# Cosine of a three-stage fused kernel: quarter turn added before rounding, absolute value dropped

## The chip, the cores and the metric

One core of a Trainium2 chip runs the whole program. The metric is device time in microseconds (us) of one execution, median of 3 runs. The core's engines run their own instruction streams in order and wait for each other by semaphores: TensorE (PE in the profile, its weight loads PEld), VectorE (DVE), ScalarE (ACT), GpSimd (POOL), and SyncE (SP), which here only starts DMAs.

## The reference, cut to what matters

```
x  = chunked softmax attention(q, k, v)        # 8 batches, 8 heads, 576 tokens in chunks of 64
x  = x as 4608 tokens by 512
h  = x @ w_in            # 4608 x 2048
g  = h * cos(h)          # the line that the change touches
x  = g @ w_out           # 4608 x 512
out = ((x @ w1) * (x @ w2)) @ w3 @ w_out2
```

All arrays are fp32. The kernel multiplies w3 by w_out2 once, in parts that it calls folds, so the last layer needs a single product per tile.

## The kernel before, in words

Every matrix product is made of three matmuls (function mm3, lines 106 to 108): each operand is split into a high part, rounded to the PE's fp32r format by a ScalarE copy, and a low part, which is the difference. The tokens form 9 tiles of 512, and the 2048 hidden columns form 8 groups of 256. A group of one tile is one step of the main loop; there are 72 steps, and in each of them two tiles of 128 x 512 hidden values are made, called d and e (variable `which` 0 and 1).

The steps run in two passes. Pass 1 takes tiles 0 to 8 with groups 0 to 4 and makes attention for the next tile on the way; its sums over groups are stored as x2a. Pass 2 takes groups 5 to 7 of every tile, adds the stored sums (line 600, `x2a<-x2a,acc`, four VectorE additions after a tile's third group), and makes the folds on the way. After pass 2 comes the second feed-forward layer, in which no cosine is taken.

The first 10 steps (class Plain) multiply by 16 blocks; d and e stay in PSUM, and the tile's PSUM bank is free again when VectorE has read it for the last time, at line 562. All later steps use a scheme with seven block products instead of eight (class Seven): step1 makes x1 (ScalarE copies it out of PSUM, line 481), step2 makes d (VectorE, line 489), step5 makes parts of e and the rest of d (lines 499, 501), step3 the rest of e (line 508). d and e then lie in SBUF.

The cosine of d or e is a chain over two engines, with one tile t:

- chain_t (line 547, ScalarE): t = h/2pi, written as a whole number (int32)
- chain_r (line 552, VectorE): t = h/2pi - t
- chain_cos (lines 557 and 558, ScalarE): absolute value, then sine with a scale and with half_pi (a column of 128 values) as the bias
- chain_g (line 562, VectorE): t = t * h
- split_g (lines 570 and 571): high part on ScalarE, low part on GpSimd, into g, from which x2_mm makes the sums over groups one step later

No scheduler moves anything: the order on every engine is the order of the code. It is set by strings, one letter per action, such as ORDER1PE and ORDER3: "1", "2", "5", "3" are the products, "a"/"c" chain_t of d and e, "A"/"C" chain_r, "b"/"d" chain_cos, "B"/"D" chain_g, "s" split_g of the step before, "x"/"y" x2_mm, "q" a piece of attention or a fold, "o" one of the seven operands of the next tile (a split, lines 101 and 102), "l", "m", "h", "r" the four parts of the conversion of one weight tile (raw weights come in by DMA, line 116; the first to read them are lines 253 on ScalarE and 263 on VectorE).

ScalarE's exponential (line 375, attention) and its sine are in different function tables, so a table load stands ahead of each exponential and of each first sine after one.

Of the kernel before, what the change touches and what calls it, by code (L numbers as in the profile page):

```python
# [11 lines left out]
I32 = mybir.dt.int32  # L12
U32 = mybir.dt.uint32
AF = mybir.ActivationFunctionType
# [15 lines left out]
INV2PI = 1.0 / (2.0 * math.pi)  # L30
TWO_PI = 2.0 * math.pi
# [25 lines left out]
def chunk_attention_two_ffn(  # L57
# [13 lines left out]
    nc = tc.nc  # L71
# [20 lines left out]
    half_pi = cpool.tile([P, 1], F32, name="half_pi")  # L92
# [451 lines left out]
    def chain_t(i, h, which):  # L544

        rr[i, which] = t = wk.tile([P, TT], F32, tag="t", name="t")
        nc.scalar.activation(t.bitcast(I32), h, AF.Copy, scale=INV2PI)  # L547

    def chain_r(i, h, which):

# [3 lines left out]
    def chain_cos(i, which):  # L554

        t = rr[i, which]
        nc.scalar.activation(t, t, AF.Abs)  # L557
        nc.scalar.activation(t, t, AF.Sin, scale=-TWO_PI, bias=half_pi)  # L558

    def chain_g(i, h, which):  # L560
        t = rr[i, which]
# [194 lines left out]
    with tc.manual_schedule():  # L756
# [34 lines left out]
        for i in range(NG):  # L791
# [35 lines left out]
            for op in order_of(i, nth, end):  # L827
# [24 lines left out]
                elif op == "r":  # L852
                    st_lo()
                elif op in "1253PQ":
                    getattr(z, "step" + op)()
                elif op in "ac":
                    chain_t(i, z.d if op == "a" else z.e, "ac".index(op))
                elif op in "AC":
                    chain_r(i, z.d if op == "A" else z.e, "AC".index(op))
                elif op in "bd":  # L860
                    chain_cos(i, "bd".index(op))
                elif op in "BD":
                    chain_g(i, z.d if op == "B" else z.e, "BD".index(op))
                elif op == "q":
                    if i < iA and nth < 4:
                        att_tok(steps[20 * n + 5 * nth + n_q], False)
                    elif i >= iB + FOLD and fq < 4 * FB2:
                        need(("w3", fq // 2), *(("wo2", j) for j in range(FB2)))
                        fold(fq // 4, fq % 4)
                        fq += 1  # L870
                        if fq == 4 * FB2:
                            load_wf(0)
                            load_wf(1)
                    n_q += 1
                elif op in "ST":
                    x_sums("ST".index(op))
                elif op == "o":
                    if i < GA and not n_o:
                        x_plain()
                    x_op((z.done if i < GA or i >= 2 * GA else OPS)[n_o], n + 1 if ps == 0 else None)  # L880
                    n_o += 1
# [138 lines left out]
```

## Time and profile before

| what | value |
|---|---|
| median of 3 runs | 1510.13 us (1508.39 to 1510.74) |
| the profiled execution | 1515.81 us |
| its span, first to last instruction | 1514.0 us |
| busy share of the span | PE 96%, PEld 83%, DVE 73%, ACT 51%, POOL 17% |
| mean granted TensorE clock | 0.994 |

A busy time is the time in which at least one instruction of an engine runs. Matmuls of one engine overlap, since the next is started while the one before drains, so a PE that is 96% busy can still lose time between two starts. In a row of the timeline, what stands in square brackets is how long the engine sat idle ahead of it, and which engine's instruction released it. A table of waits gives for each pair of waiting and releasing instruction the total, the number of times and the longest.

### The profile page before, as it was taken

Reading aid. Unit: us, or ns where it says so; the run is one execution under the profiler, and the core shown is the slowest. Engines: PE = TensorE matmul, PEld = TensorE weight load, DVE = VectorE, ACT = ScalarE, POOL = GpSimd, SP = SyncE. Lnnn points to the kernel's source line nnn. Section 1 sums busy time; section 2 is a strip of 40 time slices with the busy share of each in tenths; the row PEclk is TensorE's granted clock in tenths of the full one; section 3 lists DMA queues with packets and bytes.
Section 4 is the critical chain, followed back from the end, with each engine's and each line's share of the span. In section 5 each row is a group of like instructions: output and inputs, shape, how many; then the busy total and the mean of one; then the engine's idle time right before and its main releaser. Section 6 shows DMA issues by size and latency. Waiting matters only on the chain.

```text
span 1514.0 us, 26149 instructions
## 1 busy us (share of the span) xinstructions
PE 1455.7 (96%) x9996; PEld 1251.1 (83%) x9996; DVE 1099.8 (73%) x1844; ACT 766.9 (51%) x1317; POOL 262.0 (17%) x194
## 2 busy tenths in 40 slices
PE   4789999999999999999999989999999999999998
PEld 4678778888888888888888878898888888888886
DVE  6986798888988887767777777776665656656553
ACT  3777788888888876555555555321122013004002
POOL 0222222222222222222222112120100200200000
PEclk9999999999999999999999999999999999999999
DMA  7664555565665626998889774596434542641501
GB/s 235 204 210 133 188 173 204 188 228 166 227 218 165 229 88 248 363 328 299 309 308 326 252 282 127 196 367 238 152 140 154 190 153 90 228 157 59 210 33 56
DMA packets 122814, 307.39 MB, mean 203 GB/s; under 512 B 13633, under 2 KB 25665, under 8 KB 121537
## 3 DMA queue, kind: packets, MB, share of 16 engines
q1 hardware_dynamic: 122688, 305.71, 58.3%
q8 instruction: 79, 1.29, 0.4%
q14 instruction: 47, 0.38, 0.1%
HBM read 210.50 MB, written 95.16 MB: 202 GB/s over the span
## 4 chain that ended last, share of the span: by engine, by line
PE 65%; ACT 12%; DVE 12%; DMA 7%; issue 2%; POOL 1%; SPq 0%; DVEq 0%; ACTq 0%; POOLq 0%
PE ps_hh L106 9%; PE acc L107 8%; PE acc L106 8%; PE acc L108 8%; PE ps_hh L108 8%; PE ps_hh L107 8%; PE ps_aa L107 4%; PE ps_aa L106 4%; PE ps_aa L108 4%; ACT t L558 2%; DMA sd<-raw 2%; ACT L375 2%; ACT t L557 2%; ACT L558 1%; POOL ex L384 1%
## 5 line engine op out<-in xcount | busy, mean ns | idle before, releaser
L571 POOL TENSOR_TENSOR g<-t,g 128x512 fp32r<-128x512 f32 x144 | 196.2, 1384 | 591.6 <-ACT g L570 517.2
L106 PE MATMUL acc<-g,w 128*128 128x512 f32 x576 | 228.6, 397 | 0.0
L107 PE MATMUL acc<-g,w 128*128 128x512 f32 x576 | 227.1, 394 | 0.1
L108 PE MATMUL acc<-g,w 128*128 128x512 f32 x576 | 225.0, 391 | 0.0
L108 PE MATMUL ps_hh<-T,w 128*128 128x256 f32 (+1 forms) x616 | 182.2, 296 | 6.3 <-DVE w L199 6.2
L106 PE MATMUL ps_hh<-T,w 128*128 128x256 f32 (+1 forms) x616 | 185.3, 301 | 0.5 <-ACT x L481 0.5
L107 PE MATMUL ps_hh<-T,w 128*128 128x256 f32 (+1 forms) x616 | 181.8, 295 | 0.0
L108 PEld LDWEIGHTS acc<-g,w 128*128 128x128 f32 x576 | 108.5, 188 | 23.3
L107 PEld LDWEIGHTS acc<-g,w 128*128 128x128 f32 x576 | 108.9, 189 | 22.3 <-POOL g L571 3.0
L108 PEld LDWEIGHTS ps_hh<-T,w 128*128 128x128 f32 x616 | 118.6, 193 | 9.4 <-DVE w L199 6.9
L106 PE MATMUL ps_hh<-B,w 128*128 128x256 f32 (+1 forms) x396 | 120.4, 304 | 5.3 <-DVE t L562 3.3
L106 PEld LDWEIGHTS acc<-g,w 128*128 128x128 f32 x576 | 108.9, 189 | 19.7
L106 PEld LDWEIGHTS ps_hh<-T,w 128*128 128x128 f32 x616 | 118.6, 192 | 6.4 <-ACT x L481 0.9
L745 ACT ACTIVATE phl<-e 128x512 fp32r<-128x512 f32 x32 | 20.2, 633 | 201.5 <-DVE e L743 201.5
L107 PEld LDWEIGHTS ps_hh<-T,w 128*128 128x128 f32 x616 | 118.6, 193 | 3.2
L107 PE MATMUL ps_hh<-B,w 128*128 128x256 f32 (+1 forms) x396 | 116.6, 294 | 0.0
L108 PE MATMUL ps_hh<-B,w 128*128 128x256 f32 (+1 forms) x396 | 116.4, 294 | 0.0
L558 ACT ACTIVATE t<-t,half_pi 128x512 f32<-128x512 f32 x144 | 104.3, 724 | 4.0
L106 PE MATMUL acc<-wf,phl 128*128 128x512 f32 x252 | 98.2, 390 | 1.5 <-DVE o L688 1.5
L107 PE MATMUL acc<-wf,phl 128*128 128x512 f32 x252 | 98.1, 389 | 0.0
L108 PE MATMUL acc<-wf,phl 128*128 128x512 f32 x252 | 98.0, 389 | 0.0
L547 ACT ACTIVATE t<-d 128x512 int32<-128x512 f32 x62 | 38.9, 628 | 115.8 <-DVE d L501 115.8
(200 smaller groups left out, 3513.8 us busy)
## 6 DMA issues: line engine op xcount, KB each, us to landing
w<-sd SPq DMA_DIRECT2D x159, 512.0 KB, 5.6
sd<-raw SPq DMA_DIRECT2D x104, 256.0 KB, 4.5
s<-sd SPq DMA_DIRECT2D x43, 256.0 KB, 4.8
qk<-in_q_dram SPq DMA_DIRECT2D x36, 256.0 KB, 4.4
qk<-in_k_dram SPq DMA_DIRECT2D x36, 256.0 KB, 4.5
vt<-in_v_dram SPq DMA_DIRECT2D x72, 128.0 KB, 3.1
x2a<-x2o SPq DMA_DIRECT2D x36, 256.0 KB, 2.6
x2a<-x2a SPq DMA_DIRECT2D x36, 256.0 KB, 6.0
```

The lines of the kernel that those rows point to most:

```text
L106: nc.tensor.matmul(ps, a[0], b[0], start=first, stop=False)
L107: nc.tensor.matmul(ps, a[0], b[1], start=False, stop=False)
L108: nc.tensor.matmul(ps, a[1], b[0], start=False, stop=last)
L375: nc.scalar.activation(ex, ex, AF.Exp, scale=SCALE)
L384: (nc.vector if early else nc.gpsimd).tensor_tensor(out=ex, in0=ex, in1=rc.unsqueeze(2).to_broadcast([P, 2 * HP, 64]), op=ALU.mult)
L547: nc.scalar.activation(t.bitcast(I32), h, AF.Copy, scale=INV2PI)
L557: nc.scalar.activation(t, t, AF.Abs)
L558: nc.scalar.activation(t, t, AF.Sin, scale=-TWO_PI, bias=half_pi)
L571: nc.gpsimd.tensor_tensor(out=lo, in0=r, in1=f32(hi), op=ALU.subtract)
L745: nc.scalar.activation(t[:, 0], e0, AF.Copy)
```

## The change

The whole number is now that of h/2pi + 1/4 and no longer that of h/2pi, which is a bias of 0.25 in the ScalarE copy that makes it. The rest h/2pi - t then lies between -3/4 and 1/4 of a turn and no longer between -1/2 and 1/2, and the sine of 2pi times the rest plus half_pi is the cosine for any of these values, with arguments from -pi to pi. The absolute value is left out, and the sine's scale changes its sign. There are two absolute values a step, 144 in all.

```diff
     def chain_t(i, h, which):
         rr[i, which] = t = wk.tile([P, TT], F32, tag="t", name="t")
-        nc.scalar.activation(t.bitcast(I32), h, AF.Copy, scale=INV2PI)
+        nc.scalar.activation(t.bitcast(I32), h, AF.Copy, scale=INV2PI, bias=0.25)

     def chain_cos(i, which):
         t = rr[i, which]
-        nc.scalar.activation(t, t, AF.Abs)
-        nc.scalar.activation(t, t, AF.Sin, scale=-TWO_PI, bias=half_pi)
+        nc.scalar.activation(t, t, AF.Sin, scale=TWO_PI, bias=half_pi)
```

The instruction order of PE, VectorE, GpSimd and SyncE is the same in both kernels, row for row; only ScalarE's differs, by the 144 rows that are gone. All lines after 557 have a number lower by one in the changed kernel: the sine is line 557 there, split_g 569 and 570.

The first place is on ScalarE in the last step of the second tile in pass 1, where the seven operands of the next tile are made between the cosines. B11, B21, T1 to T4 and B22 are these operands, xf and spare what they are made from, t_2137 and t_2139 the tiles t of d and e. Before:

```order
L101 ACTIVATE B21_167<-xf_164 128x512
L557 ACTIVATE t_2137<-t_2137 128x512
L558 ACTIVATE t_2137<-t_2137,half_pi_163 128x512
L101 ACTIVATE T2_168<-spare_165 128x512
L101 ACTIVATE T1_169<-spare_165 128x512
L557 ACTIVATE t_2139<-t_2139 128x512
L558 ACTIVATE t_2139<-t_2139,half_pi_163 128x512
L101 ACTIVATE T3_170<-xf_164 128x512
L101 ACTIVATE B22_171<-xf_164 128x512
L101 ACTIVATE T4_172<-xf_164 128x512
L481 ACTIVATE x1_2203<-ps_hh_2196 128x256
```

The same place on ScalarE in the changed kernel, where the two tiles t are called t_2119 and t_2121:

```order
L101 ACTIVATE B21_167<-xf_164 128x512
L557 ACTIVATE t_2119<-t_2119,half_pi_163 128x512
L101 ACTIVATE T2_168<-spare_165 128x512
L101 ACTIVATE T1_169<-spare_165 128x512
L557 ACTIVATE t_2121<-t_2121,half_pi_163 128x512
L101 ACTIVATE T3_170<-xf_164 128x512
L101 ACTIVATE B22_171<-xf_164 128x512
L101 ACTIVATE T4_172<-xf_164 128x512
L481 ACTIVATE x1_2183<-ps_hh_2176 128x256
```

Both absolute values are gone, and five splits and the copy of x1 each stand one or two places nearer to the front.

The second place is on ScalarE in pass 2, in the first step after a tile's end. d and e are the hidden values, x1 the first product of the next step, g what x2_mm reads. Before:

```order
L547 ACTIVATE t_8244<-d_8188 128x512
L547 ACTIVATE t_8260<-e_8241 128x512
L557 ACTIVATE t_8244<-t_8244 128x512
L558 ACTIVATE t_8244<-t_8244,half_pi_163 128x512
L557 ACTIVATE t_8260<-t_8260 128x512
L558 ACTIVATE t_8260<-t_8260,half_pi_163 128x512
L481 ACTIVATE x1_8311<-ps_hh_8304 128x256
L570 ACTIVATE g_8328<-t_8244 128x2x256
```

The same place on ScalarE in the changed kernel:

```order
L547 ACTIVATE t_8148<-d_8092 128x512
L547 ACTIVATE t_8164<-e_8145 128x512
L557 ACTIVATE t_8148<-t_8148,half_pi_163 128x512
L557 ACTIVATE t_8164<-t_8164,half_pi_163 128x512
L481 ACTIVATE x1_8213<-ps_hh_8206 128x256
L569 ACTIVATE g_8230<-t_8148 128x2x256
```

The two sines follow each other directly; each waits for VectorE's subtraction of its own tile, as the absolute value did. The copy of line 547 has the same operands in both kernels, so the bias of 0.25 is part of the instruction and no further column that is read.

## Rows read from the trace of the kernel before

**Rows 1.** Page: busy us of each engine, share of the span, instructions:

```profile
PE 1455.7 (96%) x9996; PEld 1251.1 (83%) x9996; DVE 1099.8 (73%) x1844; ACT 766.9 (51%) x1317; POOL 262.0 (17%) x194
```

**Rows 2.** Busy us of PE, PEld, DVE, ACT, POOL by stage; then clock, DMA share, GB/s:

```profile
0.00:130.00 130.00, 95.44 (x1030) 83.04 (x1031) 101.48 (x185) 82.73 (x141) 21.02 (x21) 0.96 0.58 189
...
200.00:560.00 360.00, 355.77 (x3442) 303.86 (x3441) 312.63 (x575) 295.10 (x497) 102.20 (x81) 1.00 0.58 192
...
640.00:890.00 250.00, 242.43 (x1428) 215.34 (x1427) 182.18 (x307) 130.75 (x230) 50.55 (x38) 0.99 0.88 307
```

**Rows 3.** Tile t: durations in ns (min/median/max), first and last start in us:

```profile
L557 ACT ACTIVATE t<-t x144: 612/617/637, 43.4 to 959.4; 128x512 f32<-128x512 f32 x144
L558 ACT ACTIVATE t<-t,half_pi x144: 721/724/728, 45.3 to 960.1; 128x512 f32<-128x512 f32 x144
...
L547 ACT ACTIVATE t<-d x62: 615/632/637, 192.3 to 954.6; 128x512 int32<-128x512 f32 x62
```

**Rows 4.** Waits over the whole span: us in total, times, longest us:

```profile
DVE t L562 <- ACT t L558: 37.4, 70, 3.1
...
PE ps_hh L106 <- DVE d L489: 6.8, 5, 3.0
```

**Rows 5.** Timeline of PE at six places: start, duration, idle ahead:

```profile
70.78 0.39 PE L108 MATMUL ps_hh<-T,w 128*128 128x256 f32 x1 [3.11 <-DVE w L199]
...
103.94 0.58 PE L108 MATMUL ps_hh<-T,w 128*128 128x256 f32 x1 [3.12 <-DVE w L199]
...
128.81 0.39 PE L106 MATMUL ps_hh<-B,w 128*128 128x256 f32 x1 [0.57 <-DVE t L562]
...
185.79 0.39 PE L106 MATMUL ps_hh<-B,w 128*128 128x256 f32 x1 [1.03 <-ACT x L481]
...
676.46 0.39 PE L106 MATMUL ps_hh<-B,s 128*128 128x256 f32 x1 [1.20 <-DVE d L489]
...
886.16 0.58 PE L106 MATMUL ps_hh<-B,s 128*128 128x256 f32 x1 [2.96 <-DVE d L489]
```

**Rows 6.** Timeline of ACT at a tile's end in pass 2:

```profile
669.42 0.63 ACT L547 ACTIVATE t<-e 128x512 int32<-128x512 f32 x1 [0.16 <-DVE e L508]
670.03 0.64 ACT L557 ACTIVATE t<-t 128x512 f32<-128x512 f32 x1
670.69 0.72 ACT L558 ACTIVATE t<-t,half_pi 128x512 f32<-128x512 f32 x1
...
671.97 0.72 ACT L558 ACTIVATE t<-t,half_pi 128x512 f32<-128x512 f32 x1
```

**Rows 7.** Timeline of DVE at the same place:

```profile
670.09 0.69 DVE L552 SCALAR_TENSOR_TENSOR t<-e,t 128x512 f32<-128x512 f32 x1
...
672.73 0.69 DVE L562 TENSOR_TENSOR t<-t,e 128x512 f32<-128x512 f32 x1 [0.58 <-ACT t L558]
673.34 2.47 DVE L600 TENSOR_TENSOR x2a<-x2a,acc 128x512 f32<-128x512 f32 x4
675.73 0.68 DVE L489 TENSOR_TENSOR d<-x,ps_hh 128x512 f32<-128x512 f32 x1
```

**Rows 8.** Waits of PEld from 200 to 560 us:

```profile
PEld ps_s L361 <- ACT xf L409: 1.6, 6, 0.3
```

**Rows 9.** Timeline of DVE in the first tile:

```profile
46.06 0.69 DVE L562 TENSOR_TENSOR t<-t,ps_hh 128x512 f32<-128x512 f32 x1 [0.33 <-ACT t L558]
```

**Rows 10.** Waits of PE from 570 to 965 us:

```profile
PE ps_hh L106 <- ACT x L481: 0.4, 1, 0.4
```

**Rows 11.** Waits of DVE from 570 to 965 us:

```profile
DVE cw L263 <- DMA raw<-in_w_dram: 22.3, 5, 5.2
```

**Rows 12.** Busy us and clock (third number from the end) in three short stretches:

```profile
71.00:74.00 3.00, 3.00 (x52) 2.80 (x52) 2.97 (x7) 1.68 (x3) 0.00 (x0) 1.00 0.44 147
...
104.00:107.00 3.00, 3.00 (x14) 3.00 (x15) 1.08 (x2) 0.47 (x1) 0.00 (x0) 0.50 0.94 328
...
886.00:892.00 6.00, 5.84 (x20) 5.16 (x21) 3.93 (x8) 2.71 (x5) 0.00 (x0) 0.50 1.03 406
```

## The prediction

> **What bounds the kernel now.** I read the page first: PE is busy 96% of the span, ScalarE 51% [rows 1]. The change takes work from ScalarE alone, so its worth is not ScalarE's busy time but the places where PE stands still because a cosine came late.
>
> Next the busy times by stage [rows 2]. From 200 to 560 us, where most cosines of pass 1 are made, ScalarE is busy 295 of 360 us and VectorE 313, but PE is idle for only 4.2. From 640 to 890 us PE idles 7.6 us, and in the first 130 us it idles 34.6. The last absolute value starts at 959.4 us [rows 3], so the remaining 555 us of the span have no part in this.
>
> Then the waits [rows 4]. VectorE waits 37.4 us in 70 places for a sine. This is the direct effect of the cosine's length, yet PE shows waits for few of those places. What PE waits for by way of VectorE is the first sum of the seven-product scheme (line 489, d): 6.8 us in five places, all in pass 2. The last view is the timeline around each idle piece of PE, to see whether an absolute value stands in the chain ahead of it [rows 5 to 7].
>
> **What one absolute value costs.** It lasts 617 ns [rows 3]; on the engine it takes 670.69 - 670.03 = 0.66 us from start to start [rows 6]. 144 of them by 0.62 to 0.66 us are 89 to 95 us of ScalarE, about an eighth of its work. Nothing is put in their place. The copy that rounds gets a bias: the trace has no such copy with a bias, so its cost is bounded by the two nearest rows, 632 ns for the copy without and 724 ns for the sine, which reads its bias from a column. The instruction order shows no second operand on the copy, so I take 0; the other end, 0.09 us a copy, would take 0.18 us at each place below where two copies stand in the chain. Below 0 it can't be, as the copy does all that it did. The sine now gets arguments from -pi to pi. All 144 last 721 to 728 ns whatever their data, so I take no change. The table loads stay as they are, 63 between sine and exponential in either order.
>
> **Where it lies on PE's path.** I go through the places in order of weight.
>
> *Tile ends in pass 2.* VectorE multiplies both tiles by their cosines, makes four additions to x2a (2.47 us) and only then the d that PE waits for [rows 7]. Now: the second sine starts at 671.97, its product at 672.73. After: the first sine can start when the second copy has left ScalarE, at 669.42 + 0.63 = 670.05, and lasts 0.72; the second sine waits for VectorE's subtraction, over at 670.09 + 0.69 = 670.78, and ends at 671.50, so the product starts at about 671.53. That is 1.2 us earlier. VectorE has no other wait from there to d, so d is ready 1.2 us earlier, and PE, which idles 1.20 us there [rows 5], loses all of it. The five idle pieces of PE are 1.20, 0.39, 1.09, 1.20 and 2.96 us; their sum is the 6.8 us of the table of waits. The fifth, at 886.16, is preceded by the fourth, which brings PE to it 1.2 us sooner; its releaser gets the same 1.2 us, so its length stays and I count nothing. The four others give 1.18 + 0.39 + 1.09 + 1.18 = 3.8 us.
>
> *End of the second tile, 185.79 us.* Two absolute values stand ahead of five splits and of x1 on ScalarE, and PE idles 1.03 us [rows 5]. ScalarE gives 1.3 us there, but VectorE must still do its splits and then read e out of PSUM, and it had only 0.43 + 0.35 = 0.78 us of waits to give up, and 0.1 more in front. I take 0.9.
>
> *Pass 1, 200 to 560 us.* Once in each tile the attention scores wait for a PSUM bank that ScalarE empties (xf) behind both sines: 1.6 us in six places [rows 8], of which some 0.06 us each is there at any such turn. I take 1.2. All the rest of this stage counts nothing: PE is idle 4.2 us in 360, so the cover that hides the saved 75 us of ScalarE there is PE itself.
>
> *First tiles.* At 128.81 PE idles 0.57 us for a product that waits for a sine [rows 5], with one absolute value in the chain: 0.5. In the first tile PE waits for VectorE's low parts of the weights at 70.78 and 103.94 [rows 5], and of VectorE's own waits there the cosine owns 0.33 us at 46.06 [rows 9] and as much again in the third step. I take 0.7, between 0.3 and 1.5.
>
> *The turns to the next tile at 568 and 930 us.* There PE waits directly for x1, behind two absolute values: 0.4 us at 930 [rows 10] and about half of that at 568, and the d behind it another 0.2 to 0.3 each. I take 1.0 for both.
>
> The sum is 3.8 + 0.9 + 1.2 + 0.5 + 0.7 + 1.0 = 8.1 us. The profiled execution took 1515.81 us (span 1514.0 and 1.8 around it), so it would take 1507.7. It is 5.7 us, 0.4%, above the median of the three timed runs; I carry the difference over to the median: 1510.1 - 8.1 = 1502.0 us. Less than 0.2%, some 3 us, can't be told from no change in a measurement of this kernel.
>
> **Rivals.**
>
> *More than that: the clock too.* [...] At 886 it was 0.50 for 5.84 us of work, 20 matmuls, which at full clock would have been about 2.9 us. If the pieces at 886 and 103.94 fall a little shorter, or just elsewhere, up to 2.9 + 1.5 = 4.4 us come on top: 1497.6 us. The same chance can turn against us at 70.78. [...]
>
> *Less: another wait takes the place.* In pass 2 VectorE waits 22.3 us in five places for raw weights [rows 11], with DMA busy 88% of that stage [rows 2]. If these loads keep their times, PE, now earlier, waits for them instead, and the 3.8 us are given back; in the first tiles VectorE's own work may take back the rest. What is left is 1 to 2 us: 1508.6. For it: the DMA share. Against it: SyncE issues these loads in order behind work that PE and VectorE release, which all comes earlier by as much.
>
> *Slower: raw weights later.* VectorE handles the conversion of raw weights in front of the sums that PE needs. PE has 0 to about 1 us in hand at these five places. If the earlier x2d stores and operand loads crowd the raw loads so that each lands more than 2 us later against PE, 5 x 2 less some 2 in hand eats the 8.1 us; with 3 us each the kernel is slower by about 5: 1515. For it speaks only the DMA share of 88%; against it, that the order of all DMAs is the same and nothing is added.
>
> *The bias costs as much as a column.* Then 0.18 us go at six or seven places, 1.2 us in all: 1503.2, inside the forecast.
>
> **How the numbers follow.** My forecast, 8.1 us less with its own range of 1498 to 1506 (each term between a half and one and a half, the bias's upper end in it): 0.60. The clock on top: 0.12. Less, given back: 0.21. Slower: 0.05. The bias as a column: 0.02. Faster by over 0.2% are the first, the second, the last and a little of the third: 0.76. Within 0.2%: the rest of the third and a bit of the fourth, 0.19. Slower: 0.05. The range for 8 in 10 goes from 1497 (most of the clock's case) to 1509.5 (the larger part of the third).
>
> **What the profile after would show.** ScalarE busy about 677 us, with no row of absolute values and the same 64 table loads, and the copy still at 615 to 637 ns. VectorE's waits for sines down from 37.4 to below 15 us. The idle pieces of PE for d at the four tile ends near 0, that at 886 about as long as before, and the one for x1 at the end of the second tile down to some 0.2 us. From 200 to 560 us PE idles about 3 us in place of 4.2, and the length of a step stays the same. I am wrong in the main step if PE's idle pieces at the tile ends stay, or if those for raw weights grow by what these lose; wrong on the bias if the copy gets longer; wrong on the clock if stretches at 0.50 come or go.

## The result, and the profile after

| | before | after | ratio of times, 95% interval |
|---|---|---|---|
| timed together, first | 1510.43 us (1508.39 to 1511.39, 4 runs) | 1494.84 us (1492.33 to 1496.78, 4 runs) | 0.989 [0.987, 0.991] |
| timed again | 1510.43 us (17 runs) | 1499.68 us (1492.60 to 1501.15, 6 runs) | 0.9912 [0.9889, 0.9934] |
| and again | 1510.05 us (11 runs) | 1498.40 us (1492.38 to 1499.47, 6 runs) | 0.9915 [0.9893, 0.9938] |

By the medians the change is worth 11 to 16 us. The forecast was 8.1 us, and the lower end of its range, 1497.0, lies 2 us above the first median. The two later medians lie inside the range, and so does that of all 16 runs, 1497.4. How good the forecast was is therefore read from the stages below and not from the medians. The profiled execution took 1492.33 us (span 1490.5).

Page of the kernel after, answering to [rows 1]:

```profile
PE 1444.5 (97%) x9996; PEld 1247.3 (84%) x9996; DVE 1094.4 (73%) x1844; ACT 687.4 (46%) x1173; POOL 264.7 (18%) x194
```

ScalarE lost 144 instructions and 79.5 us of busy time. TensorE's busy time fell by 11.2 us although its 9996 matmuls are the same, so a busy time holds more than work.

Tile t in the kernel after (ns min/median/max), answering to [rows 3]:

```profile
L557 ACT ACTIVATE t<-t,half_pi x144: 702/711/727, 42.2 to 937.5; 128x512 f32<-128x512 f32 x144
...
L547 ACT ACTIVATE t<-d x62: 612/632/635, 184.8 to 933.3; 128x512 int32<-128x512 f32 x62
```

The copy that rounds has its bias now and the same median as before, 632 ns. The sine is not longer for its wider arguments, 711 ns where it was 724 [rows 3].

Waits of VectorE in the kernel after, over the whole span (total us, times, longest), answering to [rows 4, 11]:

```profile
DVE d L489 <- ACT g L569: 33.8, 31, 2.2
...
DVE cw L263 <- DMA raw<-in_w_dram: 19.0, 5, 4.9
...
DVE t L561 <- ACT t L557: 3.2, 5, 2.6
```

The wait for sines went from 37.4 us in 70 places to 3.2 in 5. At line 489 VectorE now waits longer for ScalarE, 33.8 us where it was 14.0, but PE's waits for the d that is made there did not grow: over the whole span they are 3.3 us in three places where they were 6.8 in five. The wait for raw weights did not grow either.

For the rest, both kernels are cut into stages at the same seven matmuls (the 9996 matmuls have one order, so the nth of one kernel is the nth of the other). Stage lengths in us:

| stage, by the times of before | before, two profiles | after, three profiles | change | forecast |
|---|---|---|---|---|
| up to 110 | 110.2, 110.2 | 104.0, 110.4, 106.3 | see below | -0.7 |
| 110 to 200, second tile | 89.86, 89.83 | 88.49, 88.42, 88.46 | -1.4 | -1.4 |
| 200 to 560, rest of pass 1 | 360.04, 360.01 | 353.72, 353.61, 353.72 | -6.3 | -1.2 |
| 560 to 640, turn to pass 2 | 80.17, 80.14 | 79.54, 79.55, 79.54 | -0.6 | -0.4 |
| 640 to 890, tile ends of pass 2 | 249.95, 248.25 | 244.07, 244.12, 244.72 | -4.8 | -3.8 |
| 890 to 970, last turn | 79.99, 79.70 | 78.28, 77.76, 78.24 | -1.8 | -0.6 |
| 970 to 1450 | 479.91, 479.91 | 479.91, 479.91, 479.91 | 0 | 0 |

From 110 to 1450 us that makes 13.3 to 16.5 us, according to which two profiles are compared. What lies outside varies from run to run: the first 110 us by some 6 us, and what follows 1450 us took 62.5 to 66.1 us in the 13 profiles on record, with no cosine in it. The second tile came out as forecast; the rest of pass 1 did not, and it holds 5.1 us of what was missed.

The stage from 200 to 560 us: busy us of PE, PEld, DVE, ACT, POOL, with the number of instructions, then clock, DMA share, GB/s. Before, cut at these matmuls:

```profile
200.02:560.06 360.04, 355.81 (x3443) 303.90 (x3441) 312.61 (x575) 295.10 (x498) 102.26 (x81) 1.00 0.58 192
```

After:

```profile
192.51:546.23 353.72, 349.70 (x3443) 302.76 (x3442) 310.09 (x575) 265.82 (x437) 103.92 (x81) 1.00 0.58 196
```

The stage is 6.3 us shorter with the same 3443 matmuls, and PE's idle time in it is nearly the same: 360.04 - 355.81 = 4.2 before, 353.72 - 349.70 = 4.0 after. What shrank is the idle time of the weight loads: 360.04 - 303.90 = 56.1 before, 353.72 - 302.76 = 51.0 after.

### The profile page after: what moved, and what is told of

The parts are those of the page before. It is cut to its first block, busy times and chain, and to the rows that moved or that the text cites. A ratio compares the mean times of both kernels' runs of the same rounds, so it can differ in the third digit from the quotient of the medians.

```text
span 1490.5 us, 26018 instructions
## 1 busy us (share of the span) xinstructions
PE 1444.5 (97%) x9996; PEld 1247.3 (84%) x9996; DVE 1094.4 (73%) x1844; ACT 687.4 (46%) x1173; POOL 264.7 (18%) x194
## 4 chain that ended last, share of the span: by engine, by line
PE 77%; DVE 12%; ACT 4%; DMA 3%; issue 2%; POOL 1%; SPq 0%; DVEq 0%; ACTq 0%; POOLq 0%
PE acc L106 10%; PE acc L107 10%; PE acc L108 10%; PE ps_hh L106 10%; PE ps_hh L108 10%; PE ps_hh L107 9%; PE ps_aa L106 5%; PE ps_aa L107 5%; PE ps_aa L108 5%; ACT L375 2%; PE ps_v L404 1%; DVE ex L369 1%; DVE t L552 1%; POOL ex L384 1%; DVE sm L380 1%
## 5 line engine op out<-in xcount | busy, mean ns | idle before, releaser
L557 ACT ACTIVATE t<-t,half_pi 128x512 f32<-128x512 f32 x144 | 98.3, 715 | 1.4
```

What stands on the lines that cost most here:

```text
L557: nc.scalar.activation(t, t, AF.Sin, scale=TWO_PI, bias=half_pi)
```

## How a lost start hides in a busy PE

One such place in the kernel before, matmuls on PE:

```profile
265.19 0.28 PE L107 MATMUL ps_hh<-T,w 128*128 128x256 f32 x1
265.31 0.28 PE L108 MATMUL ps_hh<-T,w 128*128 128x256 f32 x1
265.65 0.96 PE L361 MATMUL ps_s<-qk 64*64 64x64 f32 x32
```

and its weight load, with the idle time ahead of it and the releaser in brackets:

```profile
265.64 0.83 PEld L361 LDWEIGHTS ps_s<-qk 64*64 64x64 f32 x32 [0.26 <-ACT xf L409]
```

A matmul of 256 columns is busy for 0.28 us, and the next is started 0.12 us after it (265.19 and 265.31). From 265.31 the next start comes 0.34 us later, so 0.22 us are lost; but the last matmul drains until 265.59, and PE is idle for only 0.06 us. That is too little for a row in PE's waits. On the weight-load row the same place shows 0.26.

Waits of the weight loads from 200 to 560 us, before (the row of ps_s is [rows 8]):

```profile
PEld ps_at L391 <- POOL ex L384: 13.5, 23, 2.2
...
PEld acc L107 <- POOL g L571: 2.0, 10, 0.2
...
PEld ps_hh L106 <- DVE d L489: 1.3, 6, 0.2
```

The same in the kernel after, 192.5 to 546.2 us:

```profile
PEld ps_at L391 <- POOL ex L384: 12.2, 23, 2.2
...
PEld ps_hh L106 <- DVE d L489: 0.4, 1, 0.4
```

The rows for xf and for g have gone, the others are smaller. Before, the four rows, that of ps_s among them, make 13.5 + 2.0 + 1.6 + 1.3 = 18.4 us, after 12.2 + 0.4 = 12.6: 5.8 us less. These tables list only the longer gaps. Compared start by start, the nth matmul of one kernel with the nth of the other, all 6.3 us lie at the same four places: 2.35 us at ps_s (xf), 1.68 at acc (g), 1.26 at ps_hh (d) and 1.05 at ps_at (ex). The granted clock is 1.00 in the stage in both kernels.

What makes xf late is its place in ScalarE's queue. Before, from the copy of pt on:

```profile
259.92 0.60 ACT L393 ACTIVATE pt<-ps_at 128x512 f32<-128x512 f32 x1
...
263.62 0.72 ACT L558 ACTIVATE t<-t,half_pi 128x512 f32<-128x512 f32 x1
264.25 1.06 ACT L595 ACTIVATE x2o<-acc 128x512 f32<-128x512 f32 x2
265.21 0.66 ACT L409 ACTIVATE xf<-ps_v 128x256 f32<-128x256 f32 x2
```

After:

```profile
251.68 0.60 ACT L393 ACTIVATE pt<-ps_at 128x512 f32<-128x512 f32 x1
...
255.79 0.66 ACT L409 ACTIVATE xf<-ps_v 128x256 f32<-128x256 f32 x2
```

From pt to xf it is 265.21 - 259.92 = 5.29 us before and 255.79 - 251.68 = 4.11 after: 1.18 us, about two absolute values, of which PE's weight load had waited 0.26.

## Experiments

Two theories: **A**, PE loses starts that its idle time doesn't show, mostly at the turn from tile to tile, where the last step of a tile puts seven operand splits on ScalarE and the next step puts x2o and xf there; against it the forecast (pass 1 hardly matters, and the rest is chance or the clock), later **D**, that every step gains alike. Then: is it the length of ScalarE's queue, or that each sine is ready sooner? In five of the kernels absolute values stay in some steps. They have a function that says which steps go without ("..." marks lines left out):

```diff
+    def without_abs(i):
+        return 2 * GA <= i < NTILE * GA
...
+        if without_abs(i):
+            nc.scalar.activation(t, t, AF.Sin, scale=TWO_PI, bias=half_pi)
+            return
         nc.scalar.activation(t, t, AF.Abs)
         nc.scalar.activation(t, t, AF.Sin, scale=-TWO_PI, bias=half_pi)
```

and chain_t has the bias 0.25 in the same steps. GA is 5, NTILE 9.

**after_again** and **after_third**: the kernel after, unchanged. **before_again**: the kernel before, a second profile.

> The changed kernel once more, for an interval and a second trace. Theory A (the gain is made of many lost starts of PE that its busy share does not show): 15 to 16 us under the kernel before, and the second trace again gains some 6 us between 200 and 560 us. Rival B (the forecast's 8.1 us plus luck of the runs): 8 to 10 us. Whatever of the two first traces' difference of 23.5 us lies ahead of the first cosine (2.2 us at 33 us) or at the last 30 us (1.5 us) should not come back.

> The changed kernel once more, in the same call as the next kernel. Expected: ratio to the kernel before 0.987 to 0.992 (12 to 19 us less). From 110 us on, the trace should agree with those of the two runs before it to within 1 us; up to 110 us it may differ by up to 5 us either way, if the variation of the first tile is one of run to run and not of the kernel.

> The kernel before, once more with a profile. If the first tile varies from run to run in this kernel as it does in the changed one, the trace differs from the first one by some us up to 110 us (the idle pieces of PE for the low parts of the weights, and the stretches at half clock behind them), and by less than 1 us from there to 1450 us.

The times and stages are in the tables above. The time of after_again, 10.7 us less, is neither A's 15 to 16 nor the forecast's 8 to 10; its trace again gains 6.4 us from 200 to 560 us, as A said. After_third came out as expected, in its ratio and, to within 0.7 us in each stage from 110 us on, in its trace. The three profiles of after agree to about 0.1 us in each stage from 110 to 640 us, and so do the two of before. What was expected of before_again missed twice. Its first 110 us are as long as in the first profile, while those of after took from 104.0 to 110.4. And from 640 to 890 us the two of before differ by 1.7 us. Of these, 1.3 us lie ahead of the long wait at 886 us, at a granted clock of 1.00. PE's waits for d, from 560 to 960 us, are

```profile
PE ps_hh L106 <- DVE d L489: 6.1, 4, 3.0
```

in the second profile, against 6.8 us in five places [rows 4], and behind the long wait, in the other 0.4 us, the half clock [rows 12] was shorter (columns as there):

```profile
885.00:891.00 6.00, 6.00 (x26) 5.30 (x26) 4.15 (x7) 3.39 (x6) 0.00 (x0) 0.72 1.03 410
```

26 matmuls at a mean clock of 0.72, against 20 at 0.50. So up to 1.7 us of the first comparison from 640 to 890 us are not the change's.

**mid_only**: without absolute values in steps 10 to 44, which is the code above.

> The absolute value is left out only in steps 10 to 44 (from about 190 to 640 us); all other steps keep the old chain. Theory A, read from the aligned starts of PE in the two traces: 6.3 us between 200 and 560 us and 0.6 us up to 625, so 6.9 us under the kernel before. Rival B (the forecast): 1.2 + 0.4 = 1.6 us. Rival C (the gain comes from the first tile, whose VectorE meets GpSimd differently): 0 to 1 us.

1502.61 us (1500.44 to 1504.41), ratio 0.994 [0.9922, 0.9958]: 7.8 us less, where by the forecast it would have been 1.6. The stage from 200 to 560 us:

```profile
195.34:548.97 353.63, 349.74 (x3442) 302.80 (x3441) 309.88 (x575) 265.62 (x437) 103.82 (x81) 1.00 0.58 196
```

All 6.4 us of the stage come from these 35 steps alone, and PE is again idle for 3.9 us. The forecast falls here, and so does C.

**pass2_only** (`return i >= NTILE * GA`) and **first10_only** (`return i < 2 * GA`).

> The absolute value is left out only in steps 45 to 71, which are pass 2. Theory A: 5.1 us up to 872 us, 0.9 at the turn at 930 and 0.8 at its end, 6.8 us in all, and up to 1.5 us more where the half-clock stretch at 886 gets shorter. Rival B (the forecast): 3.8 + 0.6 = 4.4 us. Rival C: 0 to 2 us.

> The absolute value is left out only in steps 0 to 9 (up to about 190 us). Theory A: 0.5 us at 128, 0.8 us at 186 and about 1 us in the first tile, 2.3 us; rival B (the forecast): 0.5 + 0.9 + 0.7 = 2.1 us, no different. Rival C: 8 us and more, as the aligned traces show 4 us in the first tile and 2.2 us ahead of it.

Pass2_only took 1504.30 us (1501.08 to 1505.91), ratio 0.9944 [0.9924, 0.9964]; first10_only 1509.77 us (1505.34 to 1513.82), ratio 0.9994 [0.9979, 1.0009]. Where nothing was changed the stages stayed: 359.98 and 359.97 us from 200 to 560. First10_only rules out C's 8 us and can't tell A from the forecast, which said nearly the same. Pass2_only took 243.84 us from 640 to 890 and 77.50 in the last turn; first10_only 88.42 in the second tile. PE's waits in pass 2 in pass2_only:

```profile
PE ps_hh L106 <- DVE d L489: 2.9, 1, 2.9
PE ps_hh L106 <- DVE d L501: 0.7, 2, 0.4
```

Of five waits for d the long one alone is left, as the forecast said. From 640 to 970 us pass2_only is 6.6 to 8.6 us shorter than the two profiles of before, where A had 6.8 and up to 1.5 more, and the forecast 4.4. Part of it is the clock, which stayed at 1.00 behind the long wait here. The three parts by their medians, 7.8 + 6.1 + 0.7 = 14.6 us, lie within the 13.3 to 16.5 of the stages; the whole, timed together with them as after_again, gave 10.7, with an interval of 10.0 to 16.8.

**turns_only** (within steps 10 to 44, the first and the last of each tile) and **inner_only** (the three between, with `not in` at the end). The edit of turns_only against mid_only:

```diff
-        return 2 * GA <= i < NTILE * GA
+        return 2 * GA <= i < NTILE * GA and i % GA in (0, GA - 1)
```

> The absolute value is left out only in the first and the last step of each tile, among steps 10 to 44 (15 of 35 steps, counting both ends). Theory A (in pass 1 ScalarE's queue is late only around the turn from one tile to the next, where it also makes the seven operands and empties the sums): about 1.0 of the 1.5 us a tile, so 4.5 to 6 us between the same PE instructions at 200 and 640 us. Rival D (every step gives an equal part of the 7.0 us): 14 of 35 steps, 2.8 us.

> The complement of the run above: left out only in the three inner steps of each tile, among steps 10 to 44. Theory A: the rest, 1 to 2.5 us between 200 and 640 us, through the sums of the last step that wait behind the products of the step before. Rival D: 21 of 35 steps, 4.2 us.

Turns_only took 1505.76 us (1502.76 to 1513.17), ratio 0.9975 [0.9958, 0.9992], 5.0 us less; inner_only 1506.97 us (1504.29 to 1509.85), ratio 0.9979 [0.9963, 0.9996], 3.8 less. These intervals overlap and don't tell A from D. The stage does. Turns_only:

```profile
195.88:552.05 356.17, 352.13 (x3443) 303.22 (x3441) 311.56 (x575) 282.81 (x474) 105.13 (x81) 1.00 0.57 194
```

Inner_only:

```profile
196.14:554.85 358.71, 354.26 (x3442) 303.81 (x3441) 311.26 (x575) 278.63 (x461) 100.23 (x81) 1.00 0.58 193
```

Two steps in five give 360.0 - 356.2 = 3.8 us, three give 1.3, and 1.2 of the 6.3 come only with both. With the turn up to 640 us it is 4.5 and 1.3 us; A had said 4.5 to 6 and 1 to 2.5, D 2.8 and 4.2. The other 2.5 us in inner_only's median have no stage behind them, and its first 110 us took 106.3. So D falls and A's way is right; its claim that the turns hold nearly everything is not quite.

Waits of the weight loads in the stage in turns_only, then in inner_only:

```profile
PEld ps_hh L106 <- DVE d L489: 1.8, 7, 0.4
PEld acc L107 <- POOL g L577: 1.0, 5, 0.2
```

```profile
PEld ps_s L361 <- ACT xf L409: 1.6, 6, 0.3
PEld acc L107 <- POOL g L577: 1.0, 5, 0.2
```

Xf is late when the absolute values of a tile's first and last step are there (1.6 us in inner_only, no row in turns_only), d when those of the three steps between are (1.8 us in turns_only, no row in inner_only), and g half by the one and half by the other.

**queue_filled**: the kernel after, and behind the second sine of each step six small operations on ScalarE that nobody reads.

```diff
+    idle = cpool.tile([P, 16], F32, name="idle")
...
         nc.scalar.activation(t, t, AF.Sin, scale=TWO_PI, bias=half_pi)
+        if which:
+            for _ in range(6):
+                nc.scalar.activation(idle, ident[:, 0:16], AF.Abs)
```

> The changed kernel, and behind the second sine of every step six small absolute values of a constant into a tile that nobody reads, as long on ScalarE as about one to one and a half us; the two sines stay as early as in the changed kernel. Theory Q (pass 1 gains through ScalarE's queue, that is through x1, the emptied banks and the high parts behind the sines): of the 7.0 us between 200 and 640 us at most 2 stay; pass 2 keeps the 4.5 to 5 us of its four tile ends, which come through VectorE's product, and loses the turn at 930. Rival S (what counts everywhere is the sine itself and the product that waits for it): 6 to 7 us stay in pass 1 too.

1507.86 us (1506.45 to 1510.27), ratio 0.9985 [0.9974, 0.9995]. ScalarE in this kernel, at the place shown above:

```profile
254.57 0.60 ACT L394 ACTIVATE pt<-ps_at 128x512 f32<-128x512 f32 x1
...
257.73 1.44 ACT L561 ACTIVATE idle<-ident 128x16 f32<-128x16 f32 x6
259.07 1.07 ACT L598 ACTIVATE x2o<-acc 128x512 f32<-128x512 f32 x2
260.03 0.66 ACT L410 ACTIVATE xf<-ps_v 128x256 f32<-128x256 f32 x2
```

Six take about 1.34 us, a little more than two absolute values, and from pt to xf it is 5.46 us, 0.17 more than before. The waits of the weight loads from 195 to 556 us:

```profile
PEld ps_s L362 <- ACT xf L410: 2.5, 6, 0.4
PEld acc L108 <- POOL g L574: 2.0, 10, 0.2
PEld ps_hh L107 <- DVE d L490: 1.7, 6, 0.3
```

All three are back, and ps_at is at 13.5 again. The stage from 200 to 560 us:

```profile
194.37:556.24 361.87, 356.26 (x3443) 304.21 (x3441) 310.20 (x575) 295.71 (x610) 101.88 (x81) 1.00 0.57 191
```

It is 1.8 us longer than before, and the last turn took 80.18. So in pass 1 and at the last turn, sines that are ready early keep nothing of the gain: it is the length of the queue behind them. As the filler is a little longer than what it replaces, a small share of the sines is not ruled out. From 640 to 890 us it took 245.66 and kept most of the gain; PE's waits in pass 2:

```profile
PE ps_hh L107 <- DVE d L490: 2.9, 1, 2.9
...
PE ps_hh L107 <- ACT x L482: 0.6, 2, 0.4
```

At the tile ends it is the sine that is ready sooner, as the forecast had it: four of the five waits for d stay away with a full queue, and only the direct waits for x1 return.

**product_first** and **product_later**: two steps on from the kernel after. In that kernel, from 137 to 166 us, PE idles three times 0.9 us for a product by the cosine (B), because VectorE first does a part of a weight's conversion (m).

```diff
-ORDER1P = "PsqMhQqqHaclAxqbCrRmBdyqDL"
+ORDER1P = "PsqMhQqqHaclAxqbCrRBdyqDmL"
```

Product_later keeps the old string in the first step of the second tile.

> The changed kernel with one letter of ORDER1P moved: VectorE's bits of the next weight tile (m) come behind both products instead of ahead of the first. In steps 6 to 8 PE waits 1.06 us each for that first product, whose sine is ready 0.87 us before VectorE gets to it. If the sine is no longer what is late there: about 0.85 us a step, 2.5 us less than the changed kernel by 190 us, as a second benefit of the change. If the moved conversion delays its weights' way to memory: nothing, or slower.

> As product_first (the conversion of a raw weight piece, m, stands behind the products by the cosines, B and D, and not in front of them), but only from the second step of the second tile on; the first step of that tile keeps the old order. In the trace of product_first the three pieces of PE's idle time for the product at 137, 151 and 166 us fell from about 1.06 to 0.2 us, 2.5 us in all, but a new piece of 1.7 us for the attention's normalised weights (ps_at, GpSimd) came at 138 us. If that piece comes from m being late in the first step, it goes now and the stretch from 110 to 190 us is 2.3 to 2.6 us shorter than in the changed kernel, with a time of about 2.4 us under it; if it comes from m being late in the second step, it stays and the stretch is 0.8 us shorter.

PE's waits in the second tile, in the kernel after, in product_first and in product_later:

```profile
PE ps_hh L106 <- DVE t L561: 2.9, 4, 0.9
PE ps_at L391 <- POOL ex L384: 0.6, 1, 0.6
```

```profile
PE ps_at L391 <- POOL ex L384: 2.3, 2, 1.7
PE ps_hh L106 <- DVE t L561: 0.3, 1, 0.3
```

```profile
PE ps_at L392 <- POOL ex L385: 0.6, 1, 0.6
PE ps_hh L107 <- DVE t L562: 0.3, 1, 0.3
```

(The 1.06 us of the expectation is about the weight load's wait, 1.04 us at 136.74; PE is idle for 0.9.) Product_first lost a new 1.7 us to the attention, and the tile took 87.66 us where 88.46 is after's mean: 0.8 less and not 2.5. With the late start of the swap it took 86.05, 2.4 less, as expected. The times are 1495.46 us (ratio to before 0.9901 [0.9881, 0.9921]) and 1493.30 us (1490.01 to 1499.98; 0.9894 [0.9872, 0.9917]). Against the 1498.40 us of after, timed together with it, the second is the best, but the ranges of the runs overlap; the 2.4 us are shown by the trace, not by the times.

## Why the prediction was wrong, point by point

**The step that failed** is "All the rest of this stage counts nothing: PE is idle 4.2 us in 360, so the cover … is PE itself". PE's busy time was taken for work at full speed. The stage gave 6.3 us where 1.2 were in the sum, mid_only alone gives all of them, and PE's idle time is nearly the same in both kernels: it fell by 0.2 us in this stage, that of the weight loads by 5.1. What the runs showed in its place is starts of PE that came late by 0.3 us and less each, hidden by the drain of the matmul before. The rows that point to it stood beside [rows 8]: the same table of waits has the weight loads waiting for g and d, and I priced only the row for xf. ScalarE stands in the chain of all of them. Even the row for xf was sized low: its places gave 2.35 us. The "75 us" of that sentence are wrong too; 61 absolute values went from this stage (498 instructions of ScalarE became 437), some 38 us.

**The last turn** was mis-sized: 1.8 us for 0.6. I had priced the waits for x1 and for the d behind it. The weight loads of the kernel before show two more from 925 to 968 us, for an operand split and for g:

```profile
PEld ps_aa L107 <- DVE T L102: 0.6, 1, 0.6
PEld acc L107 <- POOL g L571: 0.6, 2, 0.4
PEld ps_hh L106 <- ACT x L481: 0.6, 1, 0.6
PEld ps_hh L106 <- DVE d L489: 0.3, 1, 0.3
```

Their sum is 2.1 us; after, 0.4 for g is left, and 2.1 - 0.4 is the measured gain to 0.1.

**Tile ends of pass 2** were right in place, mechanism and size, and queue_filled shows it. Four of five waits for d went, that at 886 stayed (2.96 us in the first profile of both kernels). The sum of 3.8 came out as 3.5 to 5.9 up to 890 us, with the half clock in it. Up to the matmul at 886.16, with the clock at 1.00, the six profiles on record that have the absolute values in pass 2 took 244.2 to 246.0 us from 640 on, and the six without them and without filler 240.8 to 242.0: 3.7 us less by the means.

**The second tile**: 0.5 + 0.9 forecast, 1.4 measured. **The bias, the table loads, the sine's wider arguments**: free, as said. **First tiles**: 0.7 forecast; what happens there from run to run hides it (first10_only's interval goes from 3.2 us less to 1.4 more), so no run shows this term. ScalarE's busy time fell by 79.5 us and not by 89 to 95, because a busy time is a union and neighbouring records on ScalarE overlap: at 263.62 the sine lasts 0.72 us and the next copy starts after 0.63. The durations alone add up to 840.1 us before and 749.2 after, 90.8 less.

**The rivals.** Given back to raw weights: no, 22.3 us became 19.0. Slower: no. The clock on top (its 1.5 us are half of the 3.00 us at 0.50 from 104 us on [rows 12]): stretches at 0.50 came and went, but from run to run and in kernels of either kind. Behind the wait at 104 us the clock was 0.50 in before and in pass2_only, and that wait is gone in the first profile of after and in mid_only; behind the wait at 71 us, where before kept 1.00, it was 0.50 in after_again, which is the chance turning against the change. **What would make it wrong**: I had written that PE would idle 3 us in place of 4.2 and that a step would keep its length. The idle time stayed, and the step got shorter: that pair is what a lost start looks like.

## What to carry to other kernels

Before a stage is written off because its matmuls cover it, add up the waits of the weight loads and not PE's idle time. Here the rows for xf, g and d made 4.9 us in the kernel before, and 5.3 us came back at their matmuls; the forecast had 1.2. A row that has most of its length from elsewhere can't be priced so: of the 13.5 us of ps_at only about 1 us came back. An instruction taken from an engine that is only half busy (ScalarE, 51%) can be worth time wherever short waits of the busy engine end on that engine's queue: here the 61 absolute values that went from 200 to 560 us brought 6.3 us. And fill the queue up again with useless work of about the same length, put behind the chain: here that told the queue from the chain in one run.

## What the runs showed of the hardware

The first 110 us vary by up to 6 us from run to run. Kernels with all absolute values in the first ten steps took 105.5 to 110.2 us for them, those without 104.0 to 110.4. Which of VectorE's operations is slow there depends on when VectorE and GpSimd meet. GpSimd and VectorE in the profile of after:

```profile
65.30 2.98 POOL L570 TENSOR_TENSOR g<-t,g 128x512 fp32r<-128x512 f32 x2 [4.34 <-ACT g L569]
```

```profile
62.48 0.69 DVE L199 TENSOR_TENSOR w<-cw,w 128x512 fp32r<-128x512 f32 x1
...
65.35 1.77 DVE L199 TENSOR_TENSOR w<-cw,w 128x512 fp32r<-128x512 f32 x1
```

The same VectorE operation takes 0.69 us alone and 1.77 us while GpSimd subtracts. Not every operation is slowed: the d of line 489, which reads its second operand from PSUM, took at most 0.69 us throughout pass 1 and pass 2 of before, although 56 of the 63 had GpSimd at work for more than half of their time. In the first profile of before it was another operation that was caught, at 67.30 us, with GpSimd's subtraction starting at 67.23 (0.69 us is its median over all 20):

```profile
67.30 1.75 DVE L126 SCALAR_TENSOR_TENSOR cw<-raw,cw 128x512 uint32<-128x512 uint32 x1
```

Which one it is goes with the stalls of PE at 71 and 104 us [rows 5] in all 13 profiles. Where line 126 of the kernel before is caught ahead of the stall, the stall is 3.1 us (six profiles at 71 us, seven at 104); elsewhere it is 1.4 to 1.7 us at 71, and at 104 it is 1.9 in one profile and nearly nothing in five. What makes the two engines meet differently stays open.

At a granted clock of 1.00 matmuls of 512 columns started 0.23 us apart (1000.59 and 1000.82 in the first profile of before), at 0.50 they started 0.43 us apart (889.32 and 889.75). The granted clock did not follow the length of a stall. In the first profile of before it was 0.50 behind 3.12 us at 103.94 and 1.00 behind 3.11 us at 70.78 [rows 5, 12]. Behind the wait at 886 us, which lasted 2.96 us in both profiles of before, its mean over 6 us was 0.50 and 0.72. In product_first it was 1.00 behind 2.97 us, and in pass2_only 1.00 behind 2.85 us:

```profile
881.00:887.00 6.00, 6.00 (x32) 5.24 (x33) 5.27 (x9) 4.17 (x8) 0.00 (x0) 1.00 1.03 409
```
